# Chunked attention with a mixture layer behind it: attention in cells of 32 queries and their own 64 keys

## The chip, the cores and the metric

One core of a Trainium2 chip. The metric is the device time of one execution in microseconds (us). A core has a matrix engine (PE, TensorE), a vector engine (DVE, VectorE), an activation engine (ACT, ScalarE), a general engine (POOL, GpSimd) and a queue (SP) that issues all the transfers from memory.

## The reference

Attention over chunks of 32 queries: each chunk sees 8 memory keys, its own 32 keys, 16 to the left and 8 to the right, 64 keys in all. Behind it stands a two-layer network with a squared ReLU.

```python
B, H, S, D = 4, 8, 768, 64
chunk, left_ctx, right_ctx = (32, 16, 8)     # n_mem = 8
for c in range(S // chunk):
    ...
    k_full = np.concatenate([mem_k, k[:, :, l_start:r_end]], axis=2)
    scores = scale * np.matmul(q_c, k_full.transpose(0, 1, 3, 2))
    scores = scores - np.max(scores, axis=-1, keepdims=True)
    a = np.exp(scores)
    a = a / (np.sum(a, axis=-1, keepdims=True) + 1e-09)
    out[:, :, c_start:c_end] = np.matmul(a, v_full)
x = out.transpose(0, 2, 1, 3).reshape(B * S, H * D)      # 3072 x 512
h = x @ w_in                                             # 512 x 2048
r = np.maximum(h, 0.0)
return (s * (r * r) + b) @ w_out                         # 2048 x 512
```

All data is float32.

## The kernel before

**Chunks and steps.** The 3072 rows are cut into 8 chunks of 384 tokens (TOK). A step is one chunk and one slice `f` of 128 of the 2048 hidden columns, so there are 8 x 16 = 128 steps. Each step has a `hidden` part (12 matmuls, L602, x times w_in), four ACT passes and one DVE pass that make `gH` and `gL` (L609 to L613), and a `result` part (9 matmuls, L624, g times w_out). Numbers are split in a high part (H) and a rest (L), and three of the four products are made. Chunks 0 and 1 go together through the first slices (`PARTS = [0, 3, NF]`: chunk 0 slices 0 to 2, chunk 1 slices 0 to 2, then chunk 0 slices 3 to 15, chunk 1 slices 3 to 15); the others run one after another. Each of the 32 weight pieces (`weight`, L578 to L589) is loaded as 64-bit numbers and turned into H and L by two ACT passes and four DVE passes; ten go to tiles that are already free at the start (`early`), the others through three buffers (`words`).

**Attention.** For each chunk there are four pairs of heads (c = 0 to 3), 128 rows of data each. `product` (L437) makes the scores of blocks of 96 queries and 128 keys: 120 keys around the three chunks of the block and the 8 memory keys, so a mask (`make_mask`) shuts out the rest. `weights` (L533 to L543) is the softmax of one head: a fused DVE pass with mask and minimum per block, an exp on ACT with the sum read out (two records), a small POOL operation, a reciprocal on DVE, and the norm on POOL. The weights are then turned over: for chunks 0 and 1 by PE (`turn`, L552) and a copy to SBUF by ACT (L555) or DVE (L557), later by DVE's 32x32 transposes (`flip`, L563). `value` (L463) multiplies them with v, and `store` writes the chunk's x as H (ACT, L468) and L (DVE, L469).

**What sets the order.** A planner (`Plan.lay`) places all operations by priority, dependencies and a table of assumed durations (`HOLD`), and the engines then run what it wrote down in that order. `anchor` gives the priority of a piece of attention. Chunks 0 and 1 have their attention at the start (`alone`); from chunk 2 on it is done in **visits** between the steps: `together` puts on PE, without a break, the values of two pairs whose weights are ready and the scores of the two pairs that follow. Until the first result product PE runs filler matmuls (`warm`, L360) where it has nothing else. SP issues its transfers strictly in order, and each waits for its buffer: two buffers for `raw` (q and k), two for `v`, three for `words`.

Of the kernel before, what the change touches and what calls it, by code (L numbers as in the profile page):

```python
# [37 lines left out]
QK = TOK + GB * P  # L38
SCALE = 0.125
NEG = -2.0 ** 100  # L40
NEARLY = 16
# [6 lines left out]
BACK = 0.0  # L48
LEAD = 3.5
# [8 lines left out]
def X_AT(i, a, c):  # L58
    return 64
# [7 lines left out]
PARTS = [0, 3, NF]  # L67
# [3 lines left out]
for _u, (_, _f) in enumerate(STEPS):  # L71
    FIRST.setdefault(_f, _u)
ORDER = sorted((FIRST[f] + half, half, f) for f in range(NF) for half in range(2))
LATE_W = [x[1:] for x in ORDER[-NEARLY:]]


HOLD = dict(hidden=523, result=690, scores=245, value1=711, value2=760, scores1=970, scores2=970, turn=84, value=185, warm=215,
            relu=388, square=388, affine=565, high=388, xhigh=388, wscale=566, whigh=527, copy=270, exp=386, keep=388, store=480,
            low=555, rec=120, max=212, flip=317, xlow=500, wlow=350, wjoin=640, wsign=617, out=620,
            small=235, norm=1040, wrest=1290, issue=440)  # L80
# [198 lines left out]
def body(ctx: ExitStack, tc: tile.TileContext, qkv, w1, w2, out):  # L279
# [29 lines left out]
    early_tiles = [at(WEIGHT_AT(*LATE_W[i]), [P, 2 * DM], F32, name=f"early{i}", tag=f"slot{i}") for i in range(NEARLY)]  # L309

    def weight_tile(half, f):
        if (half, f) not in wts:
            i = LATE_W.index((half, f)) if (half, f) in LATE_W else -1
            if i < 0:
                place(WEIGHT_AT(half, f), 8 * DM)
            wts[half, f] = const.tile([P, 2, DM], F32R, name=f"w{half}_{f}", tag=f"slot{i}" if i >= 0 else f"w{half}_{f}")
        return wts[half, f]

    xr = [[at(X_AT(i, a, c), [P, TOK], F32R, name=f"x{'HL'[a]}{c}_{i}") for a in range(2) for c in range(NC_T)] for i in range(2)]
    gs = Ring([tuple(at(G_AT(i, a), [P, TOK], F32R, name=f"g{'HL'[a]}{i}") for a in range(2)) for i in range(3)])  # L320
    for half in range(2):
        for f in range(NF):
            weight_tile(half, f) if (half, f) not in LATE_W else None
# [3 lines left out]
    mask = const.tile([QB, 3, P], F32, name="mask")  # L327
# [4 lines left out]
    ts_ = ring("t", 4, [QB, GB, P], F32)  # L332
    vs_ = ring("v", 2, [P, 2 * GB * D], F32)
    aTs = ring("aT", 4, [P, GB, QB], F32)
    stats = Ring([tuple(const.tile([QB, GB], F32, name=f"{n}{i}") for n in ("nmax", "den", "rden")) for i in range(4)])
# [4 lines left out]
    def room(r, kind):  # L340
# [5 lines left out]
        few = n("s", 0) + n("v", 0) + n("S", 0) + n("V", 0)  # L346
        if kind in "SV":
            return few < 5 and r.next.get("v", 0) == len(r.vals["v"])
        if kind in "sv":
            early = not r.next.get("acc", 0)  # L350
            return n(kind, 0) < 2 + early and few < 3 + 2 * early
# [11 lines left out]
    c_id, c_aT, c_mask, c_s, c_b = (fixed() for _ in range(5))  # L363
    op("ACT", "copy", -100, lambda: nc.scalar.activation(s_sb, ones[:, :1], AF.Exp), (), (c_s[0],))
    op("POOL", "copy", -100, lambda: make_identity(nc, ident), (), (c_id[0],))
    def constants():
        for x in aTs.tiles:
            nc.gpsimd.memset(x, 0.0)

    def make_mask():  # L370

        nc.vector.memset(mask, NEG)
        for c in range(NQC):
            nc.vector.memset(mask[c * CHUNK:(c + 1) * CHUNK, :, c * CHUNK:c * CHUNK + LEFT + CHUNK + RIGHT], 0.0)
        nc.vector.memset(mask[:, 0, :LEFT], NEG)
        nc.vector.memset(mask[:, 2, CTX - RIGHT:CTX], NEG)
        nc.vector.memset(mask[:, :, CTX:P], 0.0)

    op("DVE", "wrest", -99, make_mask, (), (c_mask[0],))
    op("POOL", "wrest", 5, constants, (), (c_aT[0],))  # L380


# [16 lines left out]
    def anchor(ch, c):  # L399

        if ch == 0:
            return -30 + 2 * c
        if ch < NALONE:
            return starts[ch] - LEAD - SECOND * (H // 2 - 1 - c)
        return starts[ch] - JOIN - (8.0 if ch > NALONE else APART) * (H // 4 - c // 2)

    x_vals, open_ = {}, []

    def attend(ch, c):

# [42 lines left out]
        if alone:  # L453
            softmax()
# [255 lines left out]
```

## Time and profile before

| | |
|---|---|
| runs shown | 632.33 us median of 3 (632.15 to 632.89) |
| the profiled execution | 631.95 us |
| its span, first to last instruction | 630.2 us |
| PE busy | 620.3 us (98%), granted clock 0.999 |
| DVE, ACT, POOL busy | 359.2 us (57%), 425.1 us (67%), 86.8 us (14%) |
| steps, L602 and L624, share of the chain that ended last | 38% and 37% |
| scores L437, values L463, fillers L360, same chain | 5%, 4%, 3% |
| read from memory, written | 39.85 MB, 6.29 MB |

Busy time of an engine is the union of its instructions; matmuls overlap each other, so a busy PE says little by itself, and the time between the starts of two matmuls says more than the duration of one. The chain is followed back from the last instruction through whatever released each one.

### The profile page before, as it was taken

How to read it: one execution, taken by the hardware profiler on the slowest of the kernel's cores; microseconds unless marked ns; L12 is line 12 of the kernel's file. 1: busy time of each engine (PE TensorE's matmuls, PEld its weight loads, DVE VectorE, ACT ScalarE, POOL GpSimd, SP SyncE). 2: the span in 40 equal slices, each digit the busy share in tenths (PEclk: the TensorE clock that was granted, in tenths of full speed). 3: DMA queues.
4: the chain of work that ended last, by engine and by line, in shares of the span. 5: the costliest groups of instructions: out<-in, count | busy, mean ns of one | idle time of the engine just before them, and what ended most of it. 6: DMA issues, size and time to landing. Idle time of an engine off the chain costs nothing.

```text
span 630.2 us, 10954 instructions
## 1 busy us (share of the span) xinstructions
PE 620.3 (98%) x3854; PEld 546.6 (87%) x3854; DVE 359.2 (57%) x1283; ACT 425.1 (67%) x1140; POOL 86.8 (14%) x140
## 2 busy tenths in 40 slices
PE   9998999999999999999999999999999999999996
PEld 5677898798989899998989989898999999899995
DVE  5789998995757381755638274573817556131112
ACT  6998999966676574847658484765848476545543
POOL 4550000020211030201103020120302002000000
PEclk9999999999999999999999999999999999999999
DMA  8943445412021110212012020211103110010001
GB/s 332 405 127 91 133 153 183 167 51 86 8 93 51 48 46 1 93 51 94 0 48 97 2 93 0 93 51 38 56 0 94 51 35 0 2 51 0 1 1 50
DMA packets 17335, 46.84 MB, mean 74 GB/s; under 512 B 1920, under 2 KB 1920, under 8 KB 17280
## 3 DMA queue, kind: packets, MB, share of 16 engines
q1 hardware_dynamic: 17280, 46.15, 21.6%
q8 instruction: 30, 0.49, 0.3%
q14 instruction: 25, 0.20, 0.1%
HBM read 39.85 MB, written 6.29 MB: 73 GB/s over the span
## 4 chain that ended last, share of the span: by engine, by line
PE 87%; ACT 5%; DVE 4%; DMA 3%; issue 0%; DVEq 0%; ACTq 0%
PE ps L602 38%; PE ps L624 37%; PE ps L437 5%; PE ps L463 4%; PE ps L360 3%; DMA words<-w 3%; DVE wv L583 1%; ACT w L588 1%; ACT wv L580 1%; PE ps L552 1%; ACT ps L611 1%; DVE wv L585 1%; DVE w L589 1%; ACT ps L610 1%; ACT ps L609 1%; ACT gH L612 1%
## 5 line engine op out<-in xcount | busy, mean ns | idle before, releaser
L602 PE MATMUL ps<-xH,w 128*128 128x384 f32 x1024 | 261.2, 336 | 0.6 <-DVE w L589 0.6
L624 PE MATMUL ps<-w,gH 128*128 128x512 f32 x768 | 237.9, 391 | 0.0
L602 PEld LDWEIGHTS ps<-xH,w 128*128 128x128 f32 x1024 | 185.4, 188 | 5.1 <-DVE w L589 0.9
L613 DVE TENSOR_TENSOR gL<-ps,gH 128x384 fp32r<-128x384 f32 x128 | 71.0, 555 | 206.2 <-ACT gH L612 204.7
L602 PE MATMUL ps<-xL,w 128*128 128x384 f32 x512 | 174.0, 340 | 0.9 <-DVE gL L613 0.9
L624 PEld LDWEIGHTS ps<-w,gH 128*128 128x128 f32 x768 | 144.3, 188 | 26.4
L609 ACT ACTIVATE ps<-ps 128x384 f32<-128x384 f32 x128 | 60.8, 475 | 153.3 <-PE ps L602 152.8
L624 PE MATMUL ps<-w,gL 128*128 128x512 f32 x384 | 151.2, 394 | 1.6 <-DVE gL L613 1.6
L563 DVE STREAM_TRANSPOSE aT<-t 32x128 f32<-32x128 f32 x384 | 116.2, 302 | 26.4 <-POOL t L543 19.3
L537 ACT ACTIVATE t<-t,nmax 96x128 f32<-96x128 f32 x256 | 99.1, 389 | 13.9 <-DVE nmax L533 13.9
L602 PEld LDWEIGHTS ps<-xL,w 128*128 128x128 f32 x512 | 96.0, 188 | 8.0 <-DVE gL L613 1.3
L611 ACT ACTIVATE ps<-ps,b_sb,s_sb 128x384 f32<-128x384 f32 x128 | 82.4, 644 | 4.1
L624 PEld LDWEIGHTS ps<-w,gL 128*128 128x128 f32 x384 | 72.0, 187 | 14.7 <-DVE gL L613 3.1
L540 POOL TENSOR_SCALAR rden<-den 96x4 f32<-96x4 f32 x64 | 17.0, 266 | 408.6 <-ACT t L537 393.2
L543 POOL TENSOR_TENSOR t<-t,rden 96x512 f32<-96x512 f32 x64 | 67.4, 1062 | 28.8 <-DVE rden L542 28.6
L612 ACT ACTIVATE gH<-ps 128x384 fp32r<-128x384 f32 x128 | 63.0, 492 | 4.0
L610 ACT ACTIVATE ps<-ps 128x384 f32<-128x384 f32 x128 | 60.8, 475 | 4.0
L533 DVE CUSTOM_DVE_ANT_0 t<-ps,mask 96x128 f32<-96x128 f32 x256 | 56.7, 281 | 5.3 <-PE ps L437 4.6
L537 ACT ACTIVATION_READ_ACCUMULATOR t<-t,nmax 96x1 f32 x256 | 48.1, 188 | 0.0
L437 PE MATMUL ps<-raw 64*96 64x128 f32 x448 | 29.8, 276 | 0.0
L437 PEld LDWEIGHTS ps<-raw 64*96 64x96 f32 x448 | 25.3, 160 | 3.1 <-issue 0.9
L463 PEld LDWEIGHTS ps<-aT,v 128*64 128x64 f32 x448 | 19.4, 137 | 6.4 <-issue 4.2
(44 smaller groups left out, 297.9 us busy)
## 6 DMA issues: line engine op xcount, KB each, us to landing
raw<-qkv SPq DMA_DIRECT2D x28, 448.0 KB, 4.5
words<-w SPq DMA_DIRECT2D x22, 512.0 KB, 3.4
v<-qkv SPq DMA_DIRECT2D x28, 256.0 KB, 2.8
out<-partial SPq DMA_DIRECT2D x24, 256.0 KB, 2.0
early<-w SPq DMA_DIRECT2D x10, 512.0 KB, 10.1
early<-qkv SPq DMA_DIRECT2D x3, 448.0 KB, 5.9
early<-qkv SPq DMA_DIRECT2D x4, 256.0 KB, 6.4
early<-qkv SPq DMA_DIRECT2D x1, 449.0 KB, 3.3
```

Of the source, the lines that this page charges most:

```text
L437: nc.tensor.matmul(scv(n)[:, j, :], raw.tile[rows, j * QB:(j + 1) * QB], raw.tile[rows, TOK + j * P:TOK + (j + 1) * P], start=True, stop=True)
L533: op("DVE", "max", a + 0.1, lambda j=j: nc.vector.tensor_tensor_reduce(t.tile[:, j, :], scv()[:, j, :], mask[:, kind(j)], -SCALE, 3.0e38, ...
L537: op("ACT", "exp", late + 0.2, lambda j=j: nc.scalar.activation(t.tile[:, j, :], t.tile[:, j, :], AF.Exp, bias=nmax()[:, j:j + 1], scale=- ...
L543: op("POOL", "norm", late + 0.25, lambda: nc.gpsimd.tensor_tensor(t.tile, t.tile, rden().unsqueeze(2).to_broadcast([QB, GB, P]), ALU.mult) ...
L563: nc.vector.transpose(aT.tile[gg, :, cs], t.tile[cs, :, gg])
L602: nc.tensor.matmul(h.tile[:, :TOK], weight_tile(0, f)[:, wi, c * P:(c + 1) * P], x.tile[xi], start=(c == 0 and n == 0), stop=(c == NC_T - ...
L609: op("ACT", "relu", u, lambda: nc.scalar.activation(hp(), hp(), AF.Relu), (), (h[0],))
L610: op("ACT", "square", u, lambda: nc.scalar.activation(hp(), hp(), AF.Square), (), (h[0],))
L611: op("ACT", "affine", u, lambda: nc.scalar.activation(hp(), hp(), AF.Identity, scale=s_sb, bias=b_sb), (c_s[0], c_b[0]), (h[0],))
L612: op("ACT", "high", u, lambda: nc.scalar.activation(g.tile[0], hp(), AF.Copy), (h[0],), (g["H"],))
L613: op("DVE", "low", u, lambda: nc.vector.tensor_tensor(g.tile[1], hp(), g.tile[0].bitcast(F32), ALU.subtract), (h[0], g["H"]), (g["L"],))
L624: nc.tensor.matmul(acc.tile, g.tile[gi][:, t * P:(t + 1) * P], weight_tile(1, f)[:, wi, :], start=(first and n == 0), stop=(last and n == 2))
```

## The change

**Cells.** Keys are laid out for each 32 queries separately: a cell of 64 keys (16 left, 32, 8 right, 8 memory). The host writes `qkv` in that layout; a pair's q and k are 1,152 columns instead of 896, its v 768 instead of 512. No mask is left but for the keys outside the sequence, which a small memset in the scores sets to a large negative number (L418).

**Products.** `product` makes 24 products per pair of 64 rows, 32 queries and 64 keys: the two heads lie in the two halves of the rows, the three chunks of a block in three column tiles of 32, and the heads go to two banks. `value` makes 24 products per pair: from chunk 2 on with 128 rows (two cells), 32 columns of v and 64 columns streamed, of which zeros keep the two cells apart (`diags`, set once by POOL); for chunks 0 and 1 with 64 rows and 32 columns streamed.

**Softmax.** One softmax takes two pairs' cells of one head (in chunk 0 one pair's): 96 x 8 x 64 numbers. It is made of plain passes: maximum (L419) and subtraction (L420) on DVE, exp on ACT (L421), sum (L422), a small addition and a reciprocal on DVE, the norm on POOL. `flip` has 12 blocks per head for two pairs. Copies of turned weights are all on ACT.

**Loads and order.** Eight early tiles of 4 x 512 + 16 columns (which later hold both weights of a slice) instead of 16 of 2 x 512; they take chunk 0's q, k and v and the first eight weight pieces. Chunk 0's q and k are all issued before its v; chunk 1's loads stand among the first weights. `PARTS` is [0, 4, NF]. x tiles hold two pairs.

```diff
-NEARLY = 16
+NEARLY = 8
+BEFORE = 4.0
+FETCH = -4.4
...
-PARTS = [0, 3, NF]
+PARTS = [0, 4, NF]
...
+    def softmax(a, late, ch, S, t, st, rows, s_rows, fresh):
...
+        op("DVE", "edge", a + 0.1, lambda: nc.vector.memset(sv()[c * CHUNK:(c + 1) * CHUNK, b::GB, lo:hi], NEG), (), fresh)
+        op("DVE", "max" + size, a + 0.1, lambda: nc.vector.tensor_reduce(top(), sv(), axis=AX.X, op=ALU.max), fresh, (st["m", key],))
+        op("DVE", "sub" + size, a + 0.1, lambda: nc.vector.tensor_tensor(tv(), sv(), wide(top), ALU.subtract), (*fresh, st["m", key]), (t[key],))
+        op("ACT", "exp" + size, late + 0.2, lambda: nc.scalar.activation(tv(), tv(), AF.Exp, scale=SCALE), (), (t[key],))
+        op("DVE", "sum" + size, late + 0.25, lambda: nc.vector.tensor_reduce(den(), tv(), axis=AX.X, op=ALU.add), (t[key],), (st["d", key],))
+        op("DVE", "rec", late + 0.25, lambda: nc.vector.tensor_scalar(den(), den(), 1e-9, None, ALU.add), (), (st["d", key],))
+        op("DVE", "rec", late + 0.25, lambda: nc.vector.reciprocal(rden(), den()), (st["d", key],), (st["r", key],))
+        op("POOL", "norm" + size, late + 0.25, lambda: nc.gpsimd.tensor_tensor(tv(), tv(), wide(rden), ALU.mult), (st["r", key],), (t[key],), lock=True)
...
+    def flip(a, t, aT):
+
+        def block(c, r, g):
+            rows = slice(r * CELL + g * CHUNK, r * CELL + (g + 1) * CHUNK)
+            nc.vector.transpose(aT.tile[rows, :, c, r * CHUNK:(r + 1) * CHUNK],
+                                t.tile[c * CHUNK:(c + 1) * CHUNK, r::2, g * CHUNK:(g + 1) * CHUNK])
...
-        op("SP", "issue", due - 1.5, lambda: nc.sync.dma_start(v.tile, qkv[b, half, c, :, QK + 2:]), (), (v[0],), size=P * 2 * GB * D * 4)
...
-                nc.tensor.matmul(scv(n)[:, j, :], raw.tile[rows, j * QB:(j + 1) * QB],
-                                 raw.tile[rows, TOK + j * P:TOK + (j + 1) * P], start=True, stop=True)
...
+            op("SP", "issue", -20 + c if ch == 0 else FETCH + 2 + c if alone else due - 1.5 + p, lambda v=v, src=src: nc.sync.dma_start(v.tile, src[:, QK + 2:]), (), (v[0],), size=P * VW * 4)
...
+        def product(p, S, at):
+
+            raw = raws_[p]
             for j in range(GB):
...
+                for c in range(NQC):
+                    k = (j // 2 * NQC + c) * 2 + j % 2
+                    for n in range(2):
+                        rows = slice(n * D, (n + 1) * D)
+                        nc.tensor.matmul(S[n].tile[c * CHUNK:(c + 1) * CHUNK, (at * GB + j) * CELL:(at * GB + j + 1) * CELL],
+                                         raw.tile[rows, k * CHUNK:(k + 1) * CHUNK],
+                                         raw.tile[rows, TOK + k * CELL:TOK + (k + 1) * CELL], start=True, stop=True)
...
-        def value(j):
...
+        def value(p, V):
+            for m in range(2):
+                for c in range(NQC):
+                    at = lambda n: ((n * 2 + m) * NQC + c) * D
+                    for r, n in ((r, n) for r in range(2) for n in range(2)) if alone else ():
...
+                        nc.tensor.matmul(V[r].tile[n * D:(n + 1) * D, to:to + CHUNK], vals_[p].tile[rows, at(n):at(n) + D],
+                                         y.tile[rows, row, c * CHUNK:(c + 1) * CHUNK], start=True, stop=True)
+                    for n, e in ((n, e) for n in range(2) for e in range(0, D, CHUNK)) if not alone else ():
+                        to = (m * NQC + c) * 2 * CHUNK
+                        nc.tensor.matmul(V[p].tile[n * D + e:n * D + e + CHUNK, to:to + 2 * CHUNK], vals_[p].tile[:, at(n) + e:at(n) + e + CHUNK],
+                                         aT[n].tile[:, 2 * p + m, c, :], start=True, stop=True)
...
-                nc.tensor.matmul(av()[n * D:(n + 1) * D, j * QB:(j + 1) * QB],
-                                 v.tile[:, (n * GB + j) * D:(n * GB + j + 1) * D], aT[n].tile[:, j, :], start=True, stop=True)
```

**Where instructions move.** PE, the first full visit: two pairs' values and two pairs' scores (`aT` the turned weights, `v` and `raw` the loads, `ps` the banks; of each kind of product one row for each pair of operands). Before:

```order
L463 MATMUL ps_181<-aT_152,v_150 64x96
L463 MATMUL ps_181<-aT_153,v_150 64x96
L463 MATMUL ps_174<-aT_154,v_151 64x96
L463 MATMUL ps_174<-aT_155,v_151 64x96
L437 MATMUL ps_177<-raw_144 96x128
L437 MATMUL ps_179<-raw_144 96x128
L437 MATMUL ps_176<-raw_145 96x128
L437 MATMUL ps_181<-raw_145 96x128
L602 MATMUL ps_174<-xL_0_97,w_6_123 128x384
```

Now:

```order
L502 MATMUL ps_149<-aT_139,v_137 32x64 x2
L502 MATMUL ps_149<-aT_140,v_137 32x64 x2
L502 MATMUL ps_148<-aT_139,v_138 32x64 x2
L502 MATMUL ps_148<-aT_140,v_138 32x64 x2
L481 MATMUL ps_151<-raw_131 32x64
L481 MATMUL ps_150<-raw_131 32x64
L481 MATMUL ps_151<-raw_132 32x64
L481 MATMUL ps_150<-raw_132 32x64
L610 MATMUL ps_154<-xL_1_95,ww_1205 128x384
```

Each of the first eight rows stood four times before (32 products in all) and the new ones stand six times (doubled) and twelve times, 96 products. The visit comes after the 24th hidden in both.

SP, its first transfers (`early` are the tiles of the start, `w` weights). Before:

```order
L427 DMA early_91<-qkv 128x898
L423 DMA early_90<-qkv 128x896
L430 DMA early_84<-qkv 128x512
L423 DMA early_88<-qkv 128x896
L430 DMA early_84<-qkv 128x512
L423 DMA early_86<-qkv 128x896
L430 DMA early_82<-qkv 128x512 x2
L423 DMA raw_144<-qkv 128x896
L423 DMA raw_145<-qkv 128x896
L578 DMA early_62<-w 128x1024
```

Now:

```order
L466 DMA early_87<-qkv 128x1154
L463 DMA early_85<-qkv 128x1152
L463 DMA early_83<-qkv 128x1152
L463 DMA early_81<-qkv 128x1152
L469 DMA early_87<-qkv 128x768
L469 DMA early_85<-qkv 128x768
L469 DMA early_83<-qkv 128x768
L469 DMA early_81<-qkv 128x768
L586 DMA early_61<-w 128x1024 x2
L586 DMA early_66<-w 128x1024
L463 DMA raw_131<-qkv 128x1152
```

Chunk 0's q and k come ahead of its v, and three weight pieces ahead of chunk 1's first load.

DVE, the first softmaxes (`t` the weights, `nmax`, `top`, `den`, `rden` the small numbers). Before, after the mask:

```order
L533 ISA t_146,nmax_156<-ps_174,mask 96x128
L533 ISA nmax_156 96x1
L533 ISA t_147,nmax_159<-ps_175,mask 96x128
L533 ISA nmax_159 96x1
L542 RECIPROCAL rden_158<-rden_158 96x4
L557 COPY aT_152<-ps_180 128x384
```

Now:

```order
L418 MEMSET ps_147 32x16
L419 TENSOR_REDUCE top_62<-ps_147 96x4
L420 TENSOR_TENSOR t_133<-ps_147,top_62 96x256
L418 MEMSET ps_148 32x16
L419 TENSOR_REDUCE top_62<-ps_148 96x4
L420 TENSOR_TENSOR t_133<-ps_148,top_62 96x256
L422 TENSOR_REDUCE den_63<-t_133 96x4
L423 TENSOR_SCALAR den_63<-den_63 96x4
L424 RECIPROCAL rden_64<-den_63 96x4
```

The fused pass, of which four stood per head and pair, has become three passes over four blocks at once, and the sum, which ACT made, waits on DVE for the exp.

## Rows read from the trace of the kernel before

**Rows 1.** Busy us (xinstructions) of each engine by stretch, then clock, DMA share, GB/s.
```profile
core 0: us, PE busy (x) PEld busy (x) DVE busy (x) ACT busy (x) POOL busy (x), PEclk, DMA share, GB/s
4.90:38.30 33.40, 33.40 (x332) 20.98 (x329) 25.13 (x149) 29.64 (x126) 16.27 (x25) 1.00 0.92 354
38.30:58.90 20.60, 18.64 (x141) 15.18 (x139) 18.95 (x47) 18.70 (x52) 7.09 (x7) 1.00 0.37 107
58.90:125.20 66.30, 64.13 (x316) 56.57 (x316) 61.54 (x137) 62.34 (x137) 2.98 (x4) 1.00 0.47 151
125.20:553.00 427.80, 427.76 (x2691) 386.88 (x2692) 238.47 (x922) 277.50 (x759) 58.09 (x92) 1.00 0.14 47
```
**Rows 2.** Timeline of PE: start us, duration us, what; a step, and a visit.
```profile
137.65 0.34 PE L602 MATMUL ps<-xL,w 128*128 128x384 f32 x1
...
141.81 0.34 PE L602 MATMUL ps<-xL,w 128*128 128x384 f32 x1
...
150.20 1.54 PE L463 MATMUL ps<-aT,v 128*64 128x96 f32 x32
151.68 1.99 PE L437 MATMUL ps<-raw 64*96 64x128 f32 x32
153.60 0.44 PE L602 MATMUL ps<-xL,w 128*128 128x384 f32 x1
```
**Rows 3.** Groups of PE from 125.2 to 556 us: busy us, mean ns.
```profile
L437 PE MATMUL ps<-raw 64*96 64x128 f32 x352 | 21.9, 274 | 0.0
L463 PE MATMUL ps<-aT,v 128*64 128x96 f32 x384 | 18.5, 249 | 0.0
```
**Rows 4.** Timeline of PE: first, fourth and 19th hidden, in brackets what it waited for.
```profile
38.31 0.53 PE L602 MATMUL ps<-xL,w 128*128 128x384 f32 x1
...
58.94 0.44 PE L602 MATMUL ps<-xL,w 128*128 128x384 f32 x1 [0.90 <-DVE gL L613]
...
125.24 0.61 PE L602 MATMUL ps<-xH,w 128*128 128x384 f32 x2 [0.61 <-DVE w L589]
```
**Rows 5.** The chain of waits: start us, us, what; four transposes of 96 columns.
```profile
41.43 0.33 PE ps L552 x4
```
**Rows 6.** Timeline of ACT: two exps that follow each other.
```profile
6.24 0.39 ACT L537 ACTIVATE t<-t,nmax 96x128 f32<-96x128 f32 x1
...
6.63 0.39 ACT L537 ACTIVATE t<-t,nmax 96x128 f32<-96x128 f32 x1
```
**Rows 7.** Groups of ACT from 4.9 to 125.2 us: the longest piece of 512 columns.
```profile
L580 ACT ACTIVATE wv<-words 128x512 f32<-128x512 f32 x22 | 14.0, 664 | 0.7 <-DMA words<-w 0.6
```
**Rows 8.** Timeline of DVE: two fused softmax passes; gL and a weight's passes.
```profile
6.15 0.28 DVE L533 CUSTOM_DVE_ANT_0 t<-ps,mask 96x128 f32<-96x128 f32 x1
...
6.36 0.28 DVE L533 CUSTOM_DVE_ANT_0 t<-ps,mask 96x128 f32<-96x128 f32 x1
...
80.38 0.42 DVE L581 TENSOR_SCALAR words<-words 128x512 int32<-128x512 int32 x1
80.72 0.55 DVE L613 TENSOR_TENSOR gL<-ps,gH 128x384 fp32r<-128x384 f32 x1
81.18 0.68 DVE L589 TENSOR_TENSOR w<-wv,w 128x512 fp32r<-128x512 f32 x1
81.78 0.69 DVE L583 SCALAR_TENSOR_TENSOR wv<-wv,words 128x512 int32<-128x512 int32 x1
82.50 0.69 DVE L585 SCALAR_TENSOR_TENSOR wv<-words,wv 128x512 int32<-128x512 int32 x1
83.11 0.68 DVE L583 SCALAR_TENSOR_TENSOR wv<-wv,words 128x512 int32<-128x512 int32 x1
```
**Rows 9.** Groups of DVE over the whole span: a 512-column read of PSUM, a small memset.
```profile
L641 DVE COPY partial<-ps 128x512 f32<-128x512 f32 x18 | 11.8, 673 | 6.0 <-PE ps L624 6.0
...
L375 DVE MEMSET mask<- 96x16 f32 x1 | 0.1, 72 | 0.1
```
**Rows 10.** Timeline of PE: the first scores.
```profile
4.37 1.12 PE L437 MATMUL ps<-early 64*96 64x128 f32 x16
```
**Rows 11.** Groups of POOL over the whole span: the norm.
```profile
L543 POOL TENSOR_TENSOR t<-t,rden 96x512 f32<-96x512 f32 x64 | 67.4, 1062 | 28.8 <-DVE rden L542 28.6
```

More of the change, by code (lines that the diff above doesn't have):

```diff
@@ L73 @@
 ORDER = sorted((FIRST[f] + half, half, f) for f in range(NF) for half in range(2))
[L74 to L80, printed above, removed]
+LATE_F = NF - NEARLY
+HOLD = dict(hidden=523, result=690, scores=560, value1=670, value2=670, scores1=540, scores2=540, turn=84, value=1300, wrest=1000, warm=215,
+            relu=388, square=388, affine=565, high=388, xhigh=388, wscale=566, whigh=527, copy=270, exp8=570, exp4=385, keep=480, store=480,
+            low=555, rec=90, edge=90, max8=600, max4=335, sub8=600, sub4=335, sum8=600, sum4=335, flip=317, xlow=500, wlow=350, wjoin=640, wsign=617, out=620,
+            small=235, norm8=1040, norm4=560, issue=440)
 LATE = dict(PE=185, ACT=135, DVE=140, POOL=60, SP=0)
@@ L322, in body @@
         for f in range(NF):
[L323 removed]
+            weight_tile(half, f) if f < LATE_F else None
     ident = const.tile([QB, QB], F32, name="ident")
@@ new lines, in writes, with reads, values @@
+        def writes(p, V):
+            return [V[r][p] for r in range(2)] if alone else [V[p][0]]
+        def reads(p):
+            return [vals_[p][0]] + [z for y in (aT[p:p + 1] if ch == 0 else aT) for z in y.parts.values()]
+        def values():
+            V = [Val(ps, "v" if alone else "V") for _ in range(2)]
+            for p in pairs:
+                op("PE", "value", due + 0.9 if alone else due, lambda p=p: value(p, V), reads(p), writes(p, V))
+            store(V)
+            used.extend(z for y in aT for z in y.parts.values())
@@ L559, in flip @@
[L559 to L567 removed]
+            last = last_[:]
+            S = [Val(ps, "S") for _ in range(2)]
@@ new lines, in attend @@
+            V = [Val(ps, "V") for _ in range(2)] if last else []
+            chain = [op("PE", f"value{p + 1}", a - 0.05, lambda p=p: last[0](p, V), last[2](p), last[4](p, V)) for p in pairs if last]
+            chain += [op("PE", f"scores{p + 1}", a - 0.05, lambda p=p: product(p, S, p), (raws_[p][0],), (S[0][p], S[1][p])) for p in pairs]
+            for o in chain[1:]:
+                for v in o.vals:
+                    if v.ring is ps and v not in chain[0].vals:
+                        chain[0].vals.append(v)
+                        v.left += 1
@@ L570, in weight @@
+            for o, nxt in zip(chain, chain[1:]):
+                o.next = nxt
+                if o not in nxt.deps:
+                    nxt.deps.add(o)
+            if last:
+                last[1](V)
+            soft(S)
+            last_[:] = [value, store, reads, values, writes]
     def weight(i, half, f, due):
         src = (w1, w2)[half][f]
-        raw = Early(i, 0, 2 * DM) if i < NEARLY - 6 else Val(words)
+        raw = Early(i // 2, i % 2 * 2 * DM, (i % 2 + 1) * 2 * DM) if i < 2 * (NEARLY - NC_T) else Val(words)
```

323 lines of the change are left out of this document (143 added, 180 removed).

## The prediction

> **What bounds the kernel now.** I read the busy time by stretch first. From 125.2 to 553 us PE is busy 427.76 of 427.80 us, DVE 238 and ACT 278 [rows 1]: there only PE's own work counts. Before that it is otherwise: from 4.9 to 38.3 us ACT is busy 29.6 of 33.4 us, from 38.3 to 125.2 us DVE is busy 80.5 and ACT 81.0 of 86.9 us, and PE is kept warm with fillers or held up. So the kernel has two regimes, a start that ACT and DVE set, and a long stretch that PE sets, and each part of the change is priced where it falls.
>
> Second, PE's timeline. In the long stretch a step (hidden plus result) repeats every 4.16 us (137.65 to 141.81), and each visit of attention adds 3.40 us (150.20 to 153.60): 1.48 us for the value products of two head pairs, 1.92 us for the scores of two more [rows 2]. By the counts there are 11 such visits (352 records of scores, 32 each) and one with values alone [rows 3].
>
> Third, where the steps start. The first hidden is at 38.31 us, the fourth (first of chunk 1) at 58.94 us, held by DVE's gL, and the 19th, chunk 0's last, has its weight (w L589) at 125.24 us, again from DVE [rows 4]. Fifteen steps lie between the last two: 15 x 4.16 = 62.4 us of work in 66.3 us, so 3.9 us are DVE's. From there PE runs through to the end of the span at 630.2 us.
>
> **The change, part by part: the visits.** The program writes 8 value products per pair (64-column tiles, 96 columns streamed) and 8 scores products (64-row tiles, 128 streamed); each is two records in the trace. Neighbours lie in different halves of the array. A value record takes 46 ns (1.48 us for 32), while a transpose of as many columns, 96, on one tile takes 83 ns (0.33 us for 4) [rows 5]; I read that as two neighbours at work together. So a pair streams 8 x 96 / 2 = 384 columns for values in 0.74 us and 8 x 128 / 2 = 512 for scores in 0.96 us: 1.93 and 1.88 ns a column [rows 2]. The change writes 24 and 24 products of 64 columns each. Values go to four column tiles of 32: 24 x 64 / 4 = 384, still 0.74 us. Scores go to two row halves times three column tiles: 24 x 64 / 6 = 256, 0.48 us. A visit is then 2 x (0.74 + 0.48) = **2.44 us instead of 3.40, 0.96 us less, 10.6 us over 11 visits**. No row shows more than two tiles together, so both ends are kept: all four or six (2.44 us), or no more than now (values 24 x 64 / 2 = 768 columns, 1.48 us a pair; scores 768, 1.44 us; a visit of 5.84 us; it is the same if neighbours don't overlap at all and a record simply pays for its columns). I take the first, since halves in columns (values) and halves in rows (scores) come out at the same price a column, and rows and columns of tiles should then add up; the second is a rival.
>
> The shortest spacing that any small product has here is 48 ns a record (18.5 us over 384 records) [rows 3], and the change needs 2.44 / 192 = 12.7 ns. The Trainium skill (TensorE: Matmul & The Clock Gate, section "Wait — 56ns, not 53.3ns?") says that start-to-start of matmuls never drops below about 25 ns however few columns they have; by that a visit would be 192 x 25 ns = 4.8 us, and the total 637 us. No row here is short enough to show it.
>
> **The softmax on ACT.** Before, each block of 128 keys takes an exp with its accumulator read, one every 0.39 us [rows 6]. Chunks 0 and 1 have 64 of them: 25 us of the start's ACT time. After, chunk 0 has eight exps of 256 columns and chunk 1 four of 512. ACT's 512-column pieces cost at most 0.66 us [rows 7], so this is at most 12 x 0.66 = 8 us. Some 17 us leave ACT, and with that the reason why DVE stood idle 8.3 us up to 38.3 us [rows 1]. In the long stretch it is worth nothing: ACT is under PE there.
>
> **The softmax on DVE.** Before, one fused pass per block, 0.21 us each (6.15 to 6.36) [rows 8], 64 times, 13.4 us, for chunks 0 and 1. After, three plain passes (maximum, subtraction, sum), a small memset of the edge and two small operations. Prices: 512 columns 0.60 us (81.18 to 81.78), 384 columns 0.46 us, so 256 columns some 0.32 us; an operation that reads what its predecessor wrote starts 0.11 us later (0.72 against 0.61) [rows 8]; a small one 0.07 us [rows 9] plus that, 0.15 us. The largest 512-column piece, 0.67 us [rows 9], is the upper end. A head in chunk 0: 0.15 + 0.43 + 0.32 + 0.43 + 0.30 = 1.63 us, eight of them 13.0; a head in chunk 1: 0.15 + 0.71 + 0.60 + 0.71 + 0.30 = 2.5 us, four of them 10. So DVE has 23 us of softmax where it had 13.4 (and four copies at L557, 1.8 us at the price of 384 columns, which go to ACT). Here the change adds work to the busier engine; it pays only because DVE no longer waits.
>
> **When the start ends.** DVE's list up to the last xL of chunk 1, by the new order: 13.0 + 10.0 softmax, eight xL at 0.46 (3.7), four gL (1.8), and of the weights nine each of L581, L583, eight each of L585, L589 (9 x (0.34 + 0.72) + 8 x (0.61 + 0.60) = 19.2) [rows 8]: 47.7 us. It begins at about 5.2 us: scores started at 4.37 us [rows 10], the first load has 29% more bytes (1,154 columns for 898, 0.37 us at 354 GB/s [rows 1]), and the products take 0.5 us. With 1 us lost, x of chunk 1 is ready, and its first hidden, now the fifth, starts at **53.9 us**. By the same list the very first hidden is at about 25 us (13.0 + two weights 4.5 + xL 1.9 after 5.2). Data is there: 590 KB a pair is 1.7 us at that rate, while DVE needs 3.3 us a pair, and the values and the first two weights are in by 17 us (5.0 MB at that rate, from 2.5 us on). The norm on POOL stays 1.06 us per 512 columns [rows 11], 32 pieces instead of 64, beside DVE.
>
> From there to the first full visit (after the 24th hidden in both orders) are 20 steps, 83.2 us, and 1.0 us of chunk 2's first scores, which already lay ahead of 58.94 us before: 138.1 us. DVE owes some 60 us up to the weight of the 20th hidden (21 weights at 2.27, 15 gL at 0.46, two softmaxes of chunk 2 at 2.5) and PE needs 63 us to get there, so DVE's stall of 3.9 us may shrink; I keep 1.5. The visit at 150.20 us comes at 139.6: **10.6 us from the start**, between 4 (DVE still stalls, its passes at the upper end) and 13.
>
> **Sum.** 10.6 + 10.6 = 21.2 us. The profiled execution is 631.95 us on a span of 630.2, 0.38 under the median of 632.33, so 610.8; I say **611 us**. At nothing I cost: flips (12 of 0.30 us per two head pairs and head instead of 16; DVE is at 56% in the long stretch [rows 1]), 8.4 MB more of loads (DMA 14% there; if that cover went, words of weights would be late), the two memsets on POOL, the mask on DVE (before the data), value products in the start (PE has fillers there). SP issues in order: behind v of chunks 1 and 2, which now wait for PE's value products, stand the words of weight 12 on. By the list those leave at about 52 us and DVE asks for them at 57; if that cover goes, DVE waits and the 1.5 us become 4.
>
> **Rivals.** *Only the visits gain* (15%): DVE's new dependent passes, each a round trip to ACT before the sum, leave it idle as often as before, and chunk 1's first hidden stays near 59 us. For it: DVE is at 93% from 38.3 to 125.2 us [rows 1], and the change gives it more. Against: its idle time lies before 38.3 us, where ACT is full. One step more is done by then, so 616 to 621 us.
> *Slower: small tiles follow one another too slowly* (12%). One mechanism, at the visits: 192 records instead of 64, and if the array takes only two at a time, or each has a least spacing, the visit grows. The break-even is 3.40 + 10.6 / 11 = 4.36 us, 22.7 ns a record. With two at a time, 5.84 us: 11 x 2.44 = 26.8 us more, less 10.6 from the start, 648 us; at the break-even 632. For it: nothing here is seen under 48 ns [rows 3]. Against: those 48 ns are explained by columns alone. The skill's 25 ns would fall on this side, its price stands above.
> *PE without fillers* (3%): fillers end at the first result product, and PE waits more between 25 and 54 us. The granted clock stays 1.00 from 38.3 to 58.9 us with 2 us idle [rows 1]; if it fell to half, some 20 us of early work would double, but DVE sets the pace there, so 611 to 625.
>
> **How the numbers follow.** Forecast 70%, 604 to 617 us: the start gives 4 to 13 us, the visits 9 to 11 us, and up to 4 us may come from DVE's stall going wholly. The rest as above. 602 to 622 us holds the forecast and the first rival, and leaves out the slow one. Faster by over 0.2% (which is what a measurement of this kernel can tell from none): 86%; the same 2%; slower 12%, the slow tiles.
>
> **What would show it.** A visit of 2.4 to 2.7 us on PE with 96 records of values and 96 of scores; first hidden near 25 us, the first of chunk 1 near 54, the first visit near 140 us; ACT's exp under 8 us in the start; PE full after that. Wrong it would be if a visit takes over 3.4 us, if DVE is idle over 5 us before 54 us, or if words of weights hold DVE from 57 us on.

## The result, and the profile after

The changed kernel takes **625.9 us** (median of 4 runs, 625.31 to 628.48) against 632.24 us (4 runs, 631.88 to 632.89): a ratio of 0.9906, 95% interval 0.9878 to 0.9935. Faster, as forecast, but by 6.3 us where 21 were predicted, and outside the range of 602 to 622 us. The profiled execution took 625.31 us on a span of 623.5 us.

Busy time by stretch, to be laid beside [rows 1]:

```profile
core 0: us, PE busy (x) PEld busy (x) DVE busy (x) ACT busy (x) POOL busy (x), PEclk, DMA share, GB/s
4.90:38.30 33.40, 29.62 (x583) 19.24 (x576) 29.19 (x82) 17.09 (x37) 7.49 (x10) 0.95 0.91 355
38.30:125.20 86.90, 83.50 (x764) 71.78 (x764) 81.82 (x153) 73.38 (x140) 4.79 (x5) 1.00 0.55 174
125.20:553.00 427.80, 421.56 (x4167) 379.87 (x4166) 217.38 (x561) 218.42 (x419) 23.93 (x23) 1.00 0.18 60
```

In the first stretch ACT fell from 29.6 to 17.1 us and DVE rose from 25.1 to 29.2, as the prediction had it. The surprise is the third: PE, which never stood there before, now stands 6.2 us. PE's timeline says where. It answers to [rows 2] and [rows 4]:

```profile
26.39 0.44 PE L610 MATMUL ps<-xL,w 128*128 128x384 f32 x1
...
55.64 0.34 PE L610 MATMUL ps<-xL,w 128*128 128x384 f32 x1
...
57.52 0.45 PE L610 MATMUL ps<-xL,w 128*128 128x384 f32 x1 [0.67 <-DVE xL L517]
...
145.30 1.55 PE L502 MATMUL ps<-aT,v 128*32 128x64 f32 x96
146.78 0.95 PE L481 MATMUL ps<-raw 64*32 64x64 f32 x70
148.84 0.52 PE L481 MATMUL ps<-raw 64*32 64x64 f32 x26 [1.11 <-issue]
149.29 0.44 PE L610 MATMUL ps<-xL,ww 128*128 128x384 f32 x1
...
174.43 1.55 PE L502 MATMUL ps<-aT,v 128*32 128x64 f32 x96
175.91 1.22 PE L481 MATMUL ps<-raw 64*32 64x64 f32 x96
177.06 0.44 PE L610 MATMUL ps<-xL,ww 128*128 128x384 f32 x1
```

Three readings. The first hidden comes at 26.39 us (forecast 25), chunk 1's first at 55.64 (53.9). The first full visit comes at 145.30 us (139.6; before 150.20): the start gave 4.9 us, not 10.6. And the visits are of two kinds. The one at 174.43 us takes 2.63 us; the one at 145.30 takes 3.99, more than the old 3.40, because PE stops for 1.1 us after the 70th of 96 scores records. The row puts that on "issue": the engine waited for nothing that the profile shows. Of the 11 visits the 1st, 4th, 5th, 10th and 11th have such a stop (in the last it falls behind the last score). From the first visit to the end of the span it is 623.5 - 145.30 = 478.2 us, against 630.2 - 150.20 = 480.0 before: so all visits together gave 1.8 us, not 10.6.

### The profile page after: what moved, and what is told of

Read it like the earlier page. It is cut to its first block, busy times and chain, and to the rows that moved or that the text cites. A ratio compares the mean times of both kernels' runs of the same rounds, so it can differ in the third digit from the quotient of the medians.

```text
span 623.5 us, 13759 instructions
## 1 busy us (share of the span) xinstructions
PE 605.3 (97%) x5854; PEld 532.3 (85%) x5861; DVE 341.3 (55%) x816; ACT 343.7 (55%) x660; POOL 37.2 (6%) x46
## 4 chain that ended last, share of the span: by engine, by line
PE 82%; DVE 11%; DMA 4%; issue 2%; ACT 1%; POOL 0%; DVEq 0%; SPq 0%; ACTq 0%
PE ps L610 37%; PE ps L633 37%; DMA words<-w 4%; PE ps L502 3%; PE ps L481 3%; DVE wv L591 2%; DVE wv L593 2%; PE ps L371 1%; DVE top L419 1%; DVE t L420 1%; DVE den L422 1%; DVE gL L622 1%; DVE w L597 1%; DVE ww L597 1%; DVE words L589 1%
## 5 line engine op out<-in xcount | busy, mean ns | idle before, releaser
L610 PE MATMUL ps<-xH,w 128*128 128x384 f32 x512 | 130.9, 336 | 0.3 <-DVE w L597 0.3
L610 PE MATMUL ps<-xH,ww 128*128 128x384 f32 x512 | 130.7, 336 | 0.0
L633 PE MATMUL ps<-w,gH 128*128 128x512 f32 x384 | 119.1, 391 | 0.0
L633 PE MATMUL ps<-ww,gH 128*128 128x512 f32 x384 | 119.0, 391 | 0.0
L610 PEld LDWEIGHTS ps<-xH,w 128*128 128x128 f32 x512 | 92.7, 188 | 3.0 <-DVE w L597 0.9
L610 PEld LDWEIGHTS ps<-xH,ww 128*128 128x128 f32 x512 | 92.8, 188 | 2.2
L610 PE MATMUL ps<-xL,w 128*128 128x384 f32 x256 | 87.4, 341 | 2.0 <-DVE top L419 1.3
L610 PE MATMUL ps<-xL,ww 128*128 128x384 f32 x256 | 86.8, 339 | 0.0
L633 PE MATMUL ps<-w,gL 128*128 128x512 f32 x192 | 76.3, 398 | 1.2 <-DVE gL L622 1.0
L633 PE MATMUL ps<-ww,gL 128*128 128x512 f32 x192 | 75.9, 395 | 1.1 <-DVE gL L622 1.1
## 6 DMA issues: line engine op xcount, KB each, us to landing
early<-w SPq DMA_DIRECT2D x8, 512.0 KB, 10.5
```

The lines of the kernel that those rows point to most:

```text
L610: nc.tensor.matmul(h.tile[:, :TOK], weight_tile(0, f)[:, wi, c * P:(c + 1) * P], xt(x, xi, c), start=(c == 0 and n == 0), stop=(c == NC_T ...
L633: nc.tensor.matmul(acc.tile, g.tile[gi][:, t * P:(t + 1) * P], weight_tile(1, f)[:, wi, :], start=(first and n == 0), stop=(last and n == 2))
```

## What the stop is

The page has a queue that carries instructions. Of the changed kernel:

```profile
PE 605.3 (97%) x5854; PEld 532.3 (85%) x5861; DVE 341.3 (55%) x816; ACT 343.7 (55%) x660; POOL 37.2 (6%) x46
...
q8 instruction: 46, 0.75, 0.5%
```

46 packets, 0.75 MB, 16 KB each; before, 30 packets. PE ran 5854 matmuls and 5861 weight loads: 11,715 / 46 = 255 a packet (before 7,708 / 30 = 257). So a packet is read as a block of 256 of PE's instructions. Counting PE's records through the trace, the stop stands at 186 past a multiple of 256 in all five visits, always at one place in a block. That place is taken here for the block's end; the trace doesn't mark it. A visit has 96 + 96 records and as many weight loads, 384 instructions. The queues during the visit with the stop (145.30 to 149.29 us):

```profile
q1 hardware_dynamic: 170, 0.47, 43.9%
q8 instruction: 1, 0.02, 1.6%
```

and during the one without (174.43 to 177.2 us), where the second queue has no row:

```profile
q1 hardware_dynamic: 55, 0.17, 25.4%
```

In the first the packet starts 1.1 us into the visit, and PE goes on 2.4 us after that. **Theory A**: PE holds the block that it works on and the next; when a block is used up, the one after the next is fetched, and if PE runs through 256 instructions (1.8 us at the pace of a visit) before that has come, it stands. Then a visit stops only if two block ends lie in it, and not where the first lies so near its beginning (31 instructions into the 9th visit, right at the start of the 3rd) that the fetch was already under way (these two packets start 1.3 and 2.2 us ahead of the visit). **Theory B**: the stop belongs to the scores products themselves.

The Trainium skill states such blocks (Runtime: NRT & Kernel Launch, section "Instruction fetch mechanics"): instruction memory is refilled in blocks of 16 KiB, 256 instructions, the next being fetched while one runs, at a cost "mostly hidden". In this trace it is hidden in the steps, where PE takes 4.16 us for 42 instructions, and is not hidden in five of eleven visits.

## Experiments on the visits

**Fewer instructions.** Values with 64 output columns, as they were before the change:

```diff
-for n, e in ((n, e) for n in range(2) for e in range(0, D, CHUNK)) if not alone else ():
-    nc.tensor.matmul(V[p].tile[n * D + e:n * D + e + CHUNK, ...], vals_[p].tile[:, at(n) + e:at(n) + e + CHUNK], ...)
+for n in range(2) if not alone else ():
+    nc.tensor.matmul(V[p].tile[n * D:(n + 1) * D, ...], vals_[p].tile[:, at(n):at(n) + D], ...)
```

> Values of the visits in 12 products of 64 output columns a pair instead of 24 of 32; everything else as in the changed kernel. A visit then is 48 records of values and 96 of scores, 288 instructions of PE with their weight loads, instead of 384. Theory A (instruction supply: PE's gap in a visit stands where PE's own instruction stream passes from one 16 KB block of 256 instructions to the next, when a block has been used up before the next has come): 288 instructions hold two block ends only if the first comes in the first 32, and then its fetch has begun before the visit, so no visit has a gap; values still take 1.48 us (the same columns over the same array), the visit 2.7 to 2.8 us everywhere, and the 5 gaps of 1.1 to 1.3 us go: 619 to 621 us. Theory B (the gap belongs to the scores products, their row halves, banks or semaphores): it stays in the same visits, 625 us. Theory C (a product of 64 columns can't share the array as one of 32 does): values take 2 x 1.48 us, 640 us.

620.31 us, ratio 0.9829 (0.9812 to 0.9846). No visit stops. Timeline of PE, the first visit:

```profile
146.32 1.62 PE L502 MATMUL ps<-aT,v 128*64 128x64 f32 x48
147.87 1.22 PE L481 MATMUL ps<-raw 64*32 64x64 f32 x96
149.02 0.44 PE L610 MATMUL ps<-xL,ww 128*128 128x384 f32 x1
```

2.70 us, and all eleven are alike. From first visit to end 618.4 - 146.32 = 472.1 us, 6.1 less than with the stops: 1.2 us for each of five. B and C fall.

**The burst in two.** The scores one step after the values:

```diff
-chain += [op("PE", f"scores{p + 1}", a - 0.05, ...) for p in pairs]
+chain2 = [op("PE", f"scores{p + 1}", a + 0.95, ...) for p in pairs]
```

> Products as in the changed kernel, but the values of a visit and its scores are no longer one chain: the scores come one step of the network later. Theory A (instruction blocks): a burst is 192 instructions and can never hold two block ends, so no gap stands in any visit; two seams instead of one cost at most 0.1 us each, 11 times: 620 to 621.5 us. Theory B (the gap belongs to the scores themselves): the scores alone still show gaps of 1.1 to 1.3 us, 625 us. Theory C (values and scores next to each other disturb one another in the array): no gap either, and values or scores get shorter than 1.48 and 1.2 us as well.

621.92 us, 0.9848 (0.9835 to 0.9862), no stop in any visit; values 1.48 us and scores 1.15 as ever, 4.3 us apart, so the two don't disturb one another (C of this run). The time lies 0.4 us above A's range; where that goes was not taken apart.

**The same work, moved in the stream.** Each filler in two halves:

```diff
-nc.tensor.matmul(idle, ones[:, :P], ones, start=True, stop=True)
+for z in range(2):
+    nc.tensor.matmul(idle[:, z * 256:z * 256 + 256], ones[:, :P], ones[:, :256], start=True, stop=True)
```

> Each filler matmul of 512 columns is written as two of 256: the same work on PE, but 69 fillers give 138 more instructions ahead of everything that follows. In the changed kernel the visits with a gap are the 1st, 4th, 5th, 10th and 11th, and the gap always stands at the same count of PE's instructions, 186 past a multiple of 256. Theory A (instruction blocks): each visit begins 138 instructions later in the stream, so the first block end falls at instruction 193, 69, 117, 165, 213, 5, 53, 101, 149, 197 and 245 of the eleven visits; the gap needs it between about 40 and 128, so it stands in the 2nd, 3rd, 7th and 8th and in no other: 623.5 to 625 us. Theory B (scores themselves) and a transfer that is in the way (the loads for the next pairs): the gaps stay in the 1st, 4th, 5th, 10th and 11th visit, 625 us.

The stops are in the 2nd, 3rd, 7th and 8th visit and in no other. Timeline of PE, the scores of these four (L482 here):

```profile
177.30 0.90 PE L482 MATMUL ps<-raw 64*32 64x64 f32 x67
179.40 0.53 PE L482 MATMUL ps<-raw 64*32 64x64 f32 x29 [1.20 <-issue]
...
214.75 1.16 PE L482 MATMUL ps<-raw 64*32 64x64 f32 x91
217.20 0.31 PE L482 MATMUL ps<-raw 64*32 64x64 f32 x5 [1.29 <-issue]
...
360.86 0.82 PE L482 MATMUL ps<-raw 64*32 64x64 f32 x59
362.79 0.63 PE L482 MATMUL ps<-raw 64*32 64x64 f32 x37 [1.11 <-issue]
...
398.25 1.09 PE L482 MATMUL ps<-raw 64*32 64x64 f32 x83
400.64 0.35 PE L482 MATMUL ps<-raw 64*32 64x64 f32 x13 [1.30 <-issue]
```

The stops stand at one count again, 193 past a multiple of 256 (this trace lacks no record; the changed kernel's lacks 7 matmuls). So the stop goes with PE's count of instructions and not with the scores or the loads: A. That PE holds just two blocks fits every visit of both runs, but no run varied it. The time, 626.53 us (0.9919, 0.9904 to 0.9935), missed the expectation: the start was 2.8 us longer (first visit at 148.07 us, more waits for gL); from there to the end it is 477.0 us, one stop less than 478.2.

**Why the scores take 1.15 us and not 0.96.** Each product of 64 keys as two of 32, on the version with wide values:

```diff
+for e in range(0, CELL, CHUNK):
     nc.tensor.matmul(S[n].tile[..., (at * GB + j) * CELL + e:(at * GB + j) * CELL + e + CHUNK],
                      raw.tile[rows, k * CHUNK:(k + 1) * CHUNK], raw.tile[rows, TOK + k * CELL + e:TOK + k * CELL + e + CHUNK], ...)
```

> On the version with wide values: each scores product of 64 keys is written as two of 32, the same columns in twice as many products (192 records a visit instead of 96). What is asked is why the scores of a visit take 1.15 us, 12.0 ns a record, and not the forecast 0.96 us (10 ns, six tiles together at the price a column of the old kernel). Theory F (a record of this kind has a least spacing, whatever it streams): 192 records x 12 ns = 2.3 us before any gap. Theory G (columns: five tiles' worth at a time): a record of 32 columns takes 6 ns, the scores again 1.15 us. Both: with 480 instructions a visit every visit now holds a block end with an unfinished fetch, gaps of over 1 us come back in most visits; first visit near 146 us; 630 to 645 us by F, 627 to 633 us by G.

667.71 us (one run). Timeline of PE, chunk 2's first scores, and those of the first visit:

```profile
75.29 2.08 PE L482 MATMUL ps<-raw 64*32 64x32 f32 x192
...
159.27 1.68 PE L482 MATMUL ps<-raw 64*32 64x32 f32 x150
163.81 0.66 PE L482 MATMUL ps<-raw 64*32 64x32 f32 x42 [2.87 <-issue]
```

192 records in 2.01 us (75.29 to 77.30), 10.5 ns each, where half the columns would be 6 ns (G) and a fixed spacing 12 (F): nearer F. Half the columns took only 1.5 ns off a record, so most of its time comes with the record. That is the error in the price: it counted columns alone, 10 ns a record at six tiles. What in a record takes the time was not taken apart; each has a weight load of its own as well. The total went beyond what either theory gave, since the stops, here up to 3.5 us, were longer, the start was 11 us longer, and the clock fell in the start and after some of the stops (last section).

## Experiments on the start

All but the first on the version with wide values (first hidden 27.37 us, chunk 1's first 56.63, first visit 146.32). Its start is the changed kernel's, so these times vary by some 1 us from run to run.

**More parts.** The change's part boundaries, first alone, then with wide values:

```diff
-PARTS = [0, 4, NF]
+PARTS = [0, 4, 10, NF]
```

> Chunks 0 and 1 share the slices in three parts (0 to 3, 4 to 9, 10 to 15) instead of two; all else as in the changed kernel. Theory D (from 55 to 126 us DVE sets the pace: a step of chunk 0 needs two new weights, 2 x 2.27 us, and one gL of 0.46 us, 5.0 us against 4.16 us of PE, twelve steps in a row): after six such steps come six that need no weight, DVE gets ahead, and PE's waits for gL from 105 to 126 us go, the wait at 82 us perhaps too: the first visit at 142.5 to 144 us instead of 145.3, 622.5 to 624 us. Theory E (what was lost after 55 us is PE's own, restarts and products of the start): first visit at 145.3 us, 625 us. If the additional sums of partial results stood in the way: over 626 us.

625.56 us, 0.9906 (0.9890 to 0.9923). First visit at 144.37 us, 0.9 earlier: the waits for gL after 105 us went, the one at 81 us stayed; less than D gave, and the time is the changed kernel's.

> Wide values together with the three parts of the slices (0 to 3, 4 to 9, 10 to 15). The parts alone brought the first visit from 145.30 to 144.37 us, with the waits for gL after 105 us gone. If the two add up: first visit 145 to 145.5 us instead of 146.3, 619 to 620 us; if the start only varies from run to run by that much: 620 to 621 us.

618.14 us, 0.9786 (0.9771 to 0.9800): **the fastest version that leaves nothing out**, first visit at 145.40. That is below the 619 to 620 us expected; 0.9 of the 2.2 us lie ahead of the first visit, the rest is not explained.

> Wide values, and chunks 0 and 1 share the slices in four parts (0 to 3, 4 to 7, 8 to 11, 12 to 15). Theory D after 66 us (twelve steps in a row with two new weights each, 5.0 us of DVE against 4.16 us of PE): only four such steps in a row are left, the waits for gL after 100 us go, that at 81 us stays at most in part; first visit 1.5 to 2.5 us earlier than with wide values alone (146.3 us), 618 to 619 us. If the extra sums (DVE, 0.62 us each, 12 more of them) or the stores on ACT come into the way: 620 us or more.

618.97 us, 0.9792 (0.9765 to 0.9819): no different from three parts. Back to the old boundary, `[0, 3, NF]`:

> Wide values, and the parts put back to 0 to 2 and 3 to 15 as in the kernel before: chunk 0 has three steps, not four, ahead of chunk 1's first. If DVE works without a break up to chunk 1's x, two weights fewer (4.5 us) bring chunk 1's first hidden, now the 4th, to 52 to 53 us, but one step (4.16 us) less is done by then: first visit 145.5 to 147 us, 619.5 to 621 us, no difference. If chunk 1's x does not depend on DVE's load (theory K), its first hidden stays at 55.5 to 57 us and a step is missing: first visit 149 to 150.5 us, 623 to 625 us.

623.33 us, 0.9863 (0.9836 to 0.9889), first visit 149.92 us, in theory K's range. For K speak DVE's last passes of chunk 1's x, first with wide values alone, then with the old boundary:

```profile
57.44 1.01 DVE L517 TENSOR_TENSOR xL<-ps,xH 128x384 fp32r<-128x384 f32 x2
...
57.26 1.01 DVE L517 TENSOR_TENSOR xL<-ps,xH 128x384 fp32r<-128x384 f32 x2
```

They come 0.2 us earlier with two weights fewer (4.5 us) ahead of them. The time says less than it seems: PE then stood 2.9 us for gL, and from 63.2 to 70.0 us its granted clock was 0.50 (last section). Nine result products took 4.01 us there, 2.07 us at full clock. PE was busy 6.2 us of that stretch, so by an estimate some 3 us of the 3.6 that the first visit came later are clock, and the price of a missing step was not measured.

**The exps in blocks again.**

```diff
-op("ACT", "exp" + size, late + 0.2, lambda: nc.scalar.activation(tv(), tv(), AF.Exp, scale=SCALE), (), (t[key],))
+for m in range(n8):
+    op("ACT", "exp1", late + 0.2, lambda m=m: nc.scalar.activation(tv()[:, m, :], tv()[:, m, :], AF.Exp, scale=SCALE), (), (t[key],))
```

> On the version with wide values: the exp of chunks 0 and 1 is done block by block again (64 pieces of 64 columns instead of 12 passes of 256 and 512), nothing else. ACT gets some 64 x 0.3 = 19 us instead of 5.8 us before 56 us. Theory H (the first hidden came 12 us earlier because ACT was relieved): the first hidden goes from 27.4 us to 30 to 33 us, ACT is busy most of the time before it. Theory D (after it DVE sets the pace): chunk 1's first hidden and the first visit move by less than that where DVE had waits to give, the first visit at 147 to 152 us instead of 146.3, 621 to 626 us. If ACT did not matter: first hidden 27.4 us, first visit 146.3 us, 620.3 us.

624.09 us, 0.9883 (0.9868 to 0.9899). A miss for H: the first hidden stays at 27.61 us. But the test was smaller than meant: ACT spends 10.7 us on exps before 56 us instead of 5.8, and in the kernel before it was 24.7 us for 64 of twice the columns, with accumulator reads beside them. So 5 us of exps more don't move the first hidden; whether all of the old ones would is not shown, and what else of the new order brought it was not taken apart. The price came later, first visit at 150.97 us, in D's range; but here too PE stood (0.9, 0.9 and 1.2 us between 49.9 and 54.2) and then had a granted clock of 0.50 up to 61.0 us.

**The old load order.**

```diff
-"issue", FETCH + c if ch == 1 else at - 4
+"issue", at - 4
-"issue", -20 + c if ch == 0 else FETCH + 2 + c if alone else due - 1.5 + p
+"issue", -20 + c if ch == 0 else due - 1.5 + p
```

> On the version with wide values: the loads of chunks 0 and 1 stand in the queue where the old priorities put them (q and k of chunk 1's first pairs ahead of seven of the eight early weights, those of its second pairs and all its v behind the early weights), everything else as it was. If the early loads had slack (data lands long before DVE comes to it): first hidden 27 to 28 us, first visit 145 to 147.5 us, 619.5 to 621.5 us, no difference. If the new order carries part of the gain: the weights of the first steps or chunk 1's second pairs come late, DVE or PE stand before 56 us, first visit 149 us or later, 623 us or more. A gain of 1 us is possible as well, since chunk 1's first scores can start earlier and DVE waited up to 1.3 us for the second.

623.92 us, 0.9871 (0.9844 to 0.9898), first hidden 29.76, first visit 150.69 us: with the old order of the loads, and what the planner makes of it, some 4 us of the gain go. By what way is open. PE stood 2.8 us ("issue") within chunk 1's first scores, where it stood 1.8 with wide values, and its granted clock was 0.50 from 26.8 to 33.7 us.

**DVE made lighter.** First without the sign pass at all, so that the planner lays everything anew:

> On the version with wide values: DVE's pass that puts the sign bit into each weight is left out (the weights lose their sign), 32 passes of 0.6 to 0.7 us, 8 of them before 56 us. Theory D (DVE sets the pace from 5 to 126 us, and with it the first visit): chunk 1's first hidden at 51 to 53 us instead of 56.6, no waits for gL after it, first visit at 136 to 139 us instead of 146.3: 610 to 613 us. Theory I (the words of the weights set the pace: three buffers, some 4 us from issue to landing): chunk 1's first hidden comes earlier, but PE still waits from 66 us on, first visit at 142 us or later, 616 us or more.

619.83 us (one run): some 22 us less of DVE, and the first visit at 146.45 us. It looked like the end of D, but the order was another one, and the granted clock was 0.50 twice for 3.4 us (from 49.9 and from 67.0 us). So the pass was cut to an eighth and the planner left in the belief that it is long:

```diff
-nc.vector.scalar_tensor_tensor(bits(), hi(), -2147483648, bits(), ALU.bitwise_and, ALU.bitwise_or)
+nc.vector.scalar_tensor_tensor(bits()[:, :64], hi()[:, :64], -2147483648, bits()[:, :64], ALU.bitwise_and, ALU.bitwise_or)
```

> On the version with wide values: the sign pass of each weight works on 64 of its 512 columns (the other columns keep no sign), and, unlike in the run without that pass, the planner still assumes the old duration, so that every engine has the same order as in the version with wide values. DVE gets 32 times some 0.45 us less, 14 us, about 3.6 of them before 56 us. Theory D (DVE's passes set the pace of the start): chunk 1's first hidden at 52.5 to 54 us instead of 56.6, no waits of PE for gL after 66 us, first visit at 140 to 142 us instead of 146.3: 614 to 616.5 us. Theory K (the order and the round trips between DVE, ACT, POOL and PE set it, and a faster DVE only waits more): chunk 1's first hidden at 55.5 us or later, first visit at 144.5 us or later, 618 us or more. In between: both, DVE after 85 us alone (its waits there are some 2 us): first visit at 143.5 to 145 us.

615.21 us, 0.9739 (0.9721 to 0.9757). Timeline of PE:

```profile
56.27 0.34 PE L610 MATMUL ps<-xL,w 128*128 128x384 f32 x1
...
141.62 1.62 PE L502 MATMUL ps<-aT,v 128*64 128x64 f32 x48
```

Both theories, one behind the other. Up to chunk 1's first hidden next to nothing is won (56.27 us for 56.63; its second half 57.31 for 58.51): K. Up to the last xL of chunk 1 the stretches of the two versions, wide values first (columns as in the first table), say why:

```profile
5.20:58.45 53.25, 46.68 (x933) 32.92 (x939) 47.55 (x119) 31.26 (x63) 11.25 (x14) 1.00 0.74 273
...
5.20:57.00 51.80, 46.87 (x939) 32.73 (x939) 43.84 (x119) 31.00 (x63) 11.26 (x14) 1.00 0.75 279
```

DVE had 3.7 us less to do and stood 8.0 us instead of 5.7. From the first hidden of chunk 1 it is 85.35 us to the first visit, where 20 steps and the scores of chunk 2 need 84.4, against 89.7 with the full pass: D, 4.3 us. What holds chunk 1's x is the chain of waits of this run (start us, us, what):

```profile
24.81 0.46 PE ps L481 x28
25.27 1.73 issue
27.00 0.43 PE ps L481 x17
27.43 3.32 PE ps L610 x18
30.75 0.69 PE ps L481 x46
...
34.64 0.60 DVE den L422
...
35.84 1.30 POOL t L425
...
41.32 1.76 PE ps L610 x9
43.08 0.69 PE ps L481 x46
...
49.89 1.05 POOL t L425
...
52.63 1.53 PE ps L498 x96
54.17 2.26 PE ps L633 x9
```

Two softmaxes in series, 31.4 to 37.1 and 43.8 to 50.9 us, each through DVE, ACT, DVE and POOL, and on PE hidden and result products queued between them. It begins with a stop of PE on "issue", 1.73 us within 48 scores, at the same count of instructions as the stops in the visits. A version that takes a piece out of this chain was not tried.

## Why the prediction was wrong

The profiled time is 14.5 us over the forecast of 610.8: 8.8 us in the visits, 5.7 in the start.

*Visits, 10.6 us forecast, 1.8 measured.* The reading of the columns was right for the values: 96 records in 1.48 us, 15.4 ns each, four tiles together. The step that failed is "a visit is then 2 x (0.74 + 0.48) = 2.44 us". First, the scores of a visit take 1.15 us instead of 0.96, records of 12.0 ns where columns alone gave 10: 2.1 us over 11 visits. Second, the sum had no term for instructions at all: 384 in one run where 128 stood before. Without stops, in the version with wide values, the visits are worth 8 us (480.0 - 472.1); the stops took 6.

*The rival of small tiles* had the right place and the wrong mechanism. Neither two tiles at a time nor a least spacing of 22.7 ns came true. The Trainium skill's least spacing of about 25 ns (TensorE: Matmul & The Clock Gate, section "Wait — 56ns, not 53.3ns?") doesn't hold for records on different tiles: here they start 12.0 and 15.4 ns apart.

*The start, 10.6 us forecast, 4.9 measured.* The prices were right: exps 5.8 us before 56 us (at most 8), DVE's softmax passes 23.4 us (23). Two steps failed. The first is "With 1 us lost, x of chunk 1 is ready, and its first hidden, now the fifth, starts at 53.9 us". The list was right in size: DVE was busy 47.7 us from its first pass at 5.47 us to the end of the last xL. But that end is at 57.46 us, since DVE stood 4.3 us, 1.3 of them for chunk 1's scores behind a stop of PE of 0.97 us ("issue"), 0.5 for ACT, the rest in gaps under 0.15 us. That chunk 1's first hidden is only 1.7 us late is in part luck: it starts on the first half of x, before the last xL is done. A lighter DVE stood longer and was hardly earlier, so DVE's list doesn't set this time. That the chain above does is read from its waits; no run took it apart. The rival *only the visits gain* had an idle DVE as well, but by round trips to ACT before the sum, and DVE has no wait there. The second is "DVE owes some 60 us up to the weight of the 20th hidden", with a stall of 1.5 us. Groups of DVE from 55.6 to 127 us:

```profile
L593 DVE SCALAR_TENSOR_TENSOR wv<-words,wv 128x512 int32<-128x512 int32 x24 | 16.6, 691 | 0.7
L591 DVE SCALAR_TENSOR_TENSOR wv<-wv,words 128x512 int32<-128x512 int32 x23 | 15.8, 687 | 0.7
...
L589 DVE TENSOR_SCALAR words<-words 128x512 int32<-128x512 int32 x23 | 9.7, 424 | 2.3 <-DMA words<-w 2.3
```

24 weights, not 21 (23 up to the 20th hidden at 123.69 us, the last up to its result): the list before had finished eight of the 32. That is 4.5 to 6.8 us more, 64 to 67 where PE needs 63. With that PE lost 5.3 us on the way to the first visit (89.66 us for 84.4), 4.3 of them DVE's by the lighter pass. The waits for words (2.3 us) are there as well, as the sentence on SP's order feared.

*Right* were the sign, the values' price, the prices of the softmax, and that PE keeps its clock from 38 us to the last steps (1.00 up to 553 us). What the rival *PE without fillers* feared, half clock once the fillers are over, came in experiments on the start instead (last section).

## What to carry to other kernels

Count instructions, not only columns: a burst of small products can run through more than a block of PE's instructions before the next has come, and each such place cost 1.2 us in the changed kernel. Where two forms stream the same columns, take the one with fewer products (48 records did what 96 did). And when an engine's list sets the pace in the sum, test it with the order held fixed: a relief of 14 us won 5 us in the order that was there, one of 22 us with an order made anew won nothing. Look at the granted clock of both runs before a difference is put down to the edit.

## What the runs showed of the hardware

A stop in a visit can cost clock too. In the version with split scores (one run) PE stood 2.71 us in the second visit, and the granted clock of the stretch around it was 0.86, part of it at 1.2 GHz:

```profile
190.00:202.00 12.00, 9.29 (x255) 8.64 (x252) 5.50 (x13) 3.92 (x8) 1.04 (x1) 0.86 0.51 167
```

The stops of 1.1 to 1.3 us in the changed kernel left it at 1.00 (third stretch of the first table).

In the start of the changed kernel the clock was 0.50 from 17.4 to 20.8 us (the 0.95 in the first stretch of that table). In three experiments on the start it fell while PE stood, and for twice as long; the rows are of the exps in blocks, the old load order and the old part boundary:

```profile
54.14:60.97 6.83, 6.73 (x107) 6.66 (x108) 6.66 (x12) 5.48 (x12) 0.74 (x1) 0.50 0.39 118
...
26.84:33.67 6.83, 6.05 (x76) 4.84 (x77) 5.47 (x13) 2.50 (x5) 1.04 (x1) 0.50 0.72 237
...
63.16:69.98 6.82, 6.20 (x16) 5.37 (x17) 5.55 (x13) 3.76 (x7) 0.00 (x0) 0.50 0.74 273
```

0.50 is 1.2 GHz. With wide values alone, and with the lighter sign pass, the clock is 1.00 in the whole start. The mean granted clock is 0.993 to 0.996 in all runs of these three and 0.997 to 0.999 with wide values, which speaks for the same in the runs that weren't profiled. The first visit came 3.6 to 4.7 us later in them; by an estimate from these rows (half of PE's busy time) up to some 3 us of each are clock. None of the three tells what its edit costs at full clock.
